# Keys projected first: a new hand-written order of the operations, and smaller tiles for the first transposes

## The chip, the core and the metric

The kernel runs on one core of a Trainium2 chip. TensorE (PE in the profile) does matrix products and transposes, VectorE (DVE) and ScalarE (ACT) elementwise work, GpSimd (POOL) elementwise work from memory alone, and SyncE (SP) issues most DMAs; ACT issues a few. Each engine runs its own instructions in order and waits on semaphores for the others. The metric is device microseconds of one execution; lower is better.

## The reference

A transformer block over `x` of 2048 tokens by 512 features, in bfloat16, with a conditioning vector `c`:

```python
mod = (_silu(c) @ w_mod).reshape(c.shape[0], 6, 1, -1)      # sa, ca, ga, sb, cb, gb
h = _layernorm(x) * (1 + ca) + sa
x = x + ga * _A_ref(h, A_wqkv, A_wo)
h = _layernorm(x) * (1 + cb) + sb
x = x + gb * _B_ref(h, B_w1, B_b1, B_w2, B_b2)
```

`_A_ref` is attention with 32 heads of 16: each token sees 8 positions, itself and every second token before it (window 8, dilation 2), with a softmax over the 8. `_B_ref` normalises once more and mixes tokens: `gelu(h^T w1 + b1) w2 + b2`, with `w1` 2048 by 1792 and `w2` 1792 by 2048.

## The kernel before

**Order.** The kernel first describes its work as a graph of named operations (`add`, `add_any`, lines 51 to 85), each with the engines that can do it. `schedule()` then emits them in the order of one long text, `ORDER` (line 180). A suffix picks the engine: `:a` ACT, `:d` DVE, `:p` POOL; without one the first alternative holds. `:q` splits a matmul into four of 32 output columns, `:s` skips. So the text fixes the order on every engine and on SP's queue. An operation that waits holds up whatever stands behind it on its engine, and a DMA waiting on SP holds up all later DMAs of SP. The text also hands out buffers: six PSUM tiles (`ps=6`, line 271), four large product buffers (`big`) and five `vD` buffers.

**Tiling.** The 16 token tiles of 128 are worked in five chunks of 2, 4, 4, 4 and 2 tiles (`SIZES`): chunk 0 is tiles 0 and 1, chunk 1 tiles 2 to 5, chunk 2 tiles 6 to 9.

**Loads and modulation.** `ld_x0`, `ld_x1` load one tile (128 KB), `ld_x_1_2` and its like two (256 KB). `ld_wmod1` and `ld_wmod0` (512 KB each) bring the columns for `ca` and `sa`; `modcols1` (PE) and `a1col` (DVE) make 1 + ca, `modcols0` (PE) and `sab` (DVE) make sa. `ld_wmod2` to `ld_wmod5` bring the other four parts, which `modrow`, `mrows` and `ld_row0` to `ld_row3` spread over the partitions. `ld_wqkv0`, `ld_wqkv1`, `ld_wqkv2` load the weights of queries, keys and values, 512 KB each.

**Layer norm.** `ln1s<tile>` takes a tile's statistics (DVE, one instruction of 0.6 us in a row of them; on ACT four instructions), `ln1v` aggregates them, `rstd1_<chunk>`, `rste1_` (ACT) and `nb1_` (DVE) give scale and shift, `n1_<tile>` normalises.

**Queries, keys, values.** For chunks 0 and 1 PE transposes the normalised tiles (`tr0_*`, `tr1_*`), and a copy `hT<chunk>_<k>` with the factor 1 + ca brings each block of 128 features into `hT`. These two chunks use the raw weights. Chunks 2 to 4 are transposed by DMA (`xt<tile>`) straight into `hT`, and use weights that were scaled by 1 + ca (`wsc<t>_<k>`, on DVE, ACT or POOL). There are two `hT` buffers: chunk 2 overwrites chunk 0's. The projections are `qkv<chunk>_<t><j>` with t = 0 for queries, 1 for keys, 2 for values; chunks 0 and 4 do two j in one group, so they have six groups and the others twelve. `ev<chunk>_<t><j>` copies a group out of PSUM; queries and values get a bias made from `sab` and the raw weights by `qvb0` and `qvb1` (PE) and `qvb_cp0`, `qvb_cp1` (DVE). Keys have no bias.

**Attention.** `qk<chunk>_<dlo>` (DVE) multiplies queries with eight shifted keys, 4096 products per partition (2048 for chunks 0 and 4); `red` (PE) sums them; `max`, `sub`, `exp`, `esum`, `rcp`, `rcq`, `smB` are the softmax. `a2_<chunk>_<jj>` and `vd<chunk>_<dhi>` are DMAs that rearrange the softmax and the values. `pv<chunk>_<dq>` (DVE) multiplies them, `pvacc` (PE) sums, `oev` copies. `halo_v` carries 16 values over to the next chunk.

**Second half.** `wo<tile>` (PE) and `x1_<tile>` apply `wo` and the residual; `n2`, `aff`, `afb` are the second norm with its scale and shift (DVE), `ln3s`, `ln3v`, `nb3`, `h3` the third. `mlp1_<part>_<f>_<s>` multiplies w1 with h3, which is possible as soon as the first `h3` tiles are there; `padd`, `park`, `gelu` close it, and `mlp2_<tile>`, `fin<tile>`, `st_out<tile>` finish the output.

**At the start.** PE runs matmuls on `ident` or on loaded tiles whose results nobody reads (`warm0` to `warm7`, lines 526 to 535); `WARM` gives their number, `GATE` the tile for which each waits.

The lines that make the transposes and the copies behind them:

```python
            KG = min(KT, 1024 // C)
            for k0 in range(0, KT, KG):
                s_ = _Slot("ps")
...
                        for sl in range(nt):
                            nc.tensor.transpose(trp[:, k2 * C + sl * P: k2 * C + (sl + 1) * P],
                                                h3[:, t0 + sl, (k0 + k2) * P:(k0 + k2 + 1) * P], ident[:])
```

C is the chunk's number of tokens, 256 or 512, so a PSUM tile holds four feature blocks of chunk 0 or two of chunk 1.

Of the kernel before, what the change touches and what calls it, by code (L numbers as in the profile page):

```python
# [190 lines left out]
qkv1_02 rste1_3 qkv1_21 smB0 ev1_02 ln1s14:a qkv2_00 a2_0_3 qkv2_10 red1_0 ev2_00 red1_1 a2_0_1 qk1_2 ln1v14 red1_2
ev2_10 modrow nb1_3 rstd1_4 wsc2_2:a red1_3 qkv1_22 qk2_0 vd0_0 qkv2_11 n1_11 n1_10:p max1 wsc2_1:a ev1_23 mrows
qkv1_20 a2_0_2 a2_0_0 rste1_4 ld_wo2 vd0_2 halo_v1:a ev1_22 vd0_3 biascols sub1 vd0_1 ev1_21 qkv2_03 pv0_0 pvacc0_0
ev1_20 exp1 ev2_11 ld_row2 pv0_2 nb1_4 esum1:q rcp1 rcq1 qkv2_01:q pv0_3 pvacc0_2 red2_0 n1_12 pvacc0_3 ev2_03
qkv2_13:q ld_row0 pv0_1 pvacc0_1 ev2_01 smB1 wsc2_3:a ev2_13 woq_s qkv2_12 qkv2_02 oev0_0 qkv2_22 oev0_2 ld_row1 wo0
qk2_1 wo1 ev2_12 red2_1 n1_13 vd1_3 ev2_02 x1_0 qkv2_20:q x1_1 biascols_cp qk2_3 qk2_2 ln2q0 qkv2_23:q red2_2 ln2q1
xt10 vd1_2 a2_1_0 red2_3 a2_1_3 n1_14 qkv2_21:q a2_1_1 a2_1_2 ev2_20 ln2m0 pv1_2 ev2_23 xt11 xt12 xt13 qkv3_02:q vd1_0
qkv3_11:q ln2w0 pvacc1_2 ev2_21 pv1_3 qkv3_10 rstd2_0 n1_15 rste2_0 nb2_0 qkv3_01 n2_0 max2 vd1_1 oev1_2 ev2_22 ev3_10
qkv3_13 ev3_02 n2_1:p aff0 xt14 pv1_0 ev3_11 qkv3_00 halo_v2 afb0 ev3_01 pv1_1 sub2 exp2 pvacc1_0 ev3_00 oev1_0
qkv3_20:q ev3_20 esum2:q pvacc1_3 rcp2 oev1_3 pvacc1_1 oev1_1 qk3_1 qkv3_12 rcq2 ev3_13 vd2_0 qkv3_03 ln3s1:a ev3_03  # L200
ev3_12 smB2 xt15 qkv4_10 ev4_10 ln3s0:a wo3 wo5 ld_w1_0_0 wo4 qk3_0 halo_v3:a x1_5 qk3_3 x1_4 red3_0 wo2:q x1_3
qkv4_20:q ln2q3 ln3v0 vd2_2 a2_2_0 vd2_3 qk3_2 ln3v1 x1_2 ln2q4 ln2m2 rstd3_0 ln2q5 a2_2_3 a2_2_2 a2_2_1 ln2q2
qkv4_00:q pv2_3 red3_1 qkv3_23:q vd2_1 ln2w2 red3_2 ev4_20 rstd2_2 rste3_0 qkv4_12:q ev4_12 rste2_2 qkv3_22:q pvacc2_3
red3_3 pv2_0 nb2_2 qkv4_02:q ev3_23 ev3_22 pv2_1 n2_2 ld_w1_0_512 qkv4_22:q ev4_00 pvacc2_1 pvacc2_0 n2_4 max3 sub3:q
# [6 lines left out]
mlp1_0_6_0:q oev3_0 mlp1_0_7_2:q mlp1_0_6_2:q pvacc3_2 n2_8:p mlp1_0_5_0:q mlp1_0_5_2:q oev3_2 pvacc3_1 max4 pv3_3
n2_7 vd4_1 vd4_2 ld_row3 park0_5 n2_6 aff6 mlp1_0_10_0:q oev3_1 mlp1_0_8_2:q sub4:q pvacc3_3 exp4 oev3_3 mlp1_0_10_2
esum4:d rcp4 ld_w1_0_1408 wo13 park0_6 wo12 afb6 rcq4 x1_13:d smB4 wo11 a2_4_2 wo10 x1_12:d x1_11:d ln3s7:a ln3s9:a
ln3s6 ln3s8 mlp1_0_11_0 ln3v7 mlp1_0_9_0 ln3v6 ln2q11 ln3v8 mlp1_0_9_2 ln3v9 vd4_3 mlp1_0_11_2 x1_10:d rstd3_6 rste3_6
nb3_6 h3_9:d a2_4_0 ln2q12 h3_7 a2_4_1 ln2m10 h3_8:d ln2q10 h3_6:d a2_4_3 mlp1_0_12_0 mlp1_0_12_2 mlp1_0_7_6 pv4_1
mlp1_0_8_6 park0_7 ln2w10 mlp1_0_9_6 ld_w2_4 mlp1_0_10_6 ln2m12 ln2q13 rstd2_10 pv4_0 pv4_2 park0_8 ld_w2_1 rste2_10
nb2_10 ld_w1_0_1664 ln2w12 pv4_3 pvacc4_0 n2_11 n2_10:d aff10 afb10 pvacc4_2 ln3s11 rstd2_12 pvacc4_1 oev4_0
mlp1_0_11_6:q pvacc4_3 park0_9 oev4_2 mlp1_0_12_6 rste2_12 nb2_12 wo14 park0_10 ln3s10:a n2_13:p wo15 mlp1_0_13_0
x1_14:d ln2q14 mlp1_0_13_2 big_done n2_12:d ln2m14 ld_w1_1_0 mlp1_0_13_6 ld_w1_1_640 park0_11 x1_15:d ln2w14 aff12
ln2q15 ln2m15 ln2w15 rstd2_15 rstd2_14 afb12 rste2_14 ln3v10 ln3v11 rstd3_10 rste3_10 ln3s13 nb2_14 mlp1_1_1_6 nb3_10  # L220
# [824 lines left out]
```

## Time and profile before

| | |
|---|---|
| median of 3 runs | 196.76 us (196.35 to 197.0) |
| the profiled execution | 196.38 us, of which the span 194.7 us |
| busy share of the span: PE, DVE, ACT, POOL | 96%, 83%, 63%, 13% |
| instructions | 4386 |
| HBM read, written | 22.03 MB, 2.10 MB |
| granted TensorE clock | 1.00 throughout |

All operations go through one helper, so nearly every row of the profile names line 131; tiles tell them apart. `big<-q_sb,k_f` is a product `qk`, `big<-a2sb,vD` a product `pv`, `psS<-hT,wst` or `psS<-hT,h` a projection with raw weights, `psS<-hT,w_qkv` one with scaled weights, `psS<-ident,h` a transpose, `psS<-sc,big` the modulation columns, `psS<-sab,wst` the query bias, `st<-xx` a statistic, `psS<-h,wst` the first MLP product. A row of the timeline has its start, its length, engine, operation, output and inputs, shapes, and the number of instructions merged; in brackets is how long the engine was idle before it, and what released it. PEld is the loading of weights into PE, which overlaps PE.

### The profile page before, as it was taken

Reading aid. Unit: us, or ns where it says so; the run is one execution under the profiler, and the core shown is the slowest. Engines: PE = TensorE matmul, PEld = TensorE weight load, DVE = VectorE, ACT = ScalarE, POOL = GpSimd, SP = SyncE. Lnnn points to the kernel's source line nnn. Section 1 sums busy time; section 2 is a strip of 40 time slices with the busy share of each in tenths; the row PEclk is TensorE's granted clock in tenths of the full one; section 3 lists DMA queues with packets and bytes.
Section 4 is the critical chain, followed back from the end, with each engine's and each line's share of the span. In section 5 each row is a group of like instructions: output and inputs, shape, how many; then the busy total and the mean of one; then the engine's idle time right before and its main releaser. Section 6 shows DMA issues by size and latency. Waiting matters only on the chain.

```text
span 194.7 us, 4386 instructions
## 1 busy us (share of the span) xinstructions
...
## 2 busy tenths in 40 slices
...
GB/s 169 320 364 254 231 183 164 268 219 178 226 152 262 187 236 209 29 107 388 200 271 71 146 231 258 329 340 236 319 22 30 148 27 0 210 90 56 92 83 81
DMA packets 55369, 35.94 MB, mean 185 GB/s; under 512 B 24628, under 2 KB 52788, under 8 KB 55348
## 3 DMA queue, kind: packets, MB, share of 16 engines
...
HBM read 22.03 MB, written 2.10 MB: 124 GB/s over the span
## 4 chain that ended last, share of the span: by engine, by line
PE 83%; DMA 6%; DVE 6%; SPq 2%; ACT 1%; issue 1%; POOL 0%; ACTq 0%
PE psS L131 79%; PE psL L131 3%; DVE big L131 2%; DMA vD<-v_sb 2%; DMA w_qkv<-in_B_w_dram 2%; DMA xx<-in_A_x_dram 2%; SPq L131 2%; DVE st L131 2%; DVE h L131 1%; DVE m L131 0%; DVE mv L131 0%; ACT xx L131 0%; ACT v_sb L131 0%; ACT o_sb L131 0%; POOL v_sb L131 0%
## 5 line engine op out<-in xcount | busy, mean ns | idle before, releaser
L131 PEld LDWEIGHTS <-wst 128*128 128x128 bf16 (+1 forms) x536 | 35.7, 100 | 32.1 <-issue 1.5
L131 PE MATMUL psS<-h,wst 128*32 128x512 bf16 (+1 forms) x374 | 51.0, 379 | 0.0
L131 DVE TENSOR_TENSOR big<-a2sb,vD 128x4096 bf16<-128x4096 bf16 (+1 forms) x20 | 36.9, 1857 | 0.6 <-DMA vD<-v_sb 0.3
L131 DVE TENSOR_TENSOR big<-q_sb,k_f 128x4096 bf16<-128x4096 bf16 (+1 forms) x20 | 36.5, 1855 | 0.0
L131 PE MATMUL psS<-hT,w_qkv 128*32 128x512 bf16 (+3 forms) x396 | 29.0, 334 | 0.1
L131 PEld LDWEIGHTS <-w_qkv 128*32 128x32 bf16 (+1 forms) x438 | 20.4, 107 | 15.4 <-issue 1.6
L131 DVE SCALAR_TENSOR_TENSOR h<-psS,bcol,rows_bc 128x512 f32<-128x512 f32 x15 | 11.3, 750 | 19.0 <-PE psS L131 18.9
L131 POOL TENSOR_SCALAR h<-xx,rs,nb 128x512 bf16<-128x512 bf16 x12 | 15.2, 1273 | 90.0 <-DVE nb L131 84.1
L131 PE MATMUL psS<-gT,big 128*128 128x512 bf16 x112 | 25.0, 379 | 0.0
L131 PEld LDWEIGHTS <-big 128*128 128x128 bf16 x144 | 12.0, 97 | 13.8 <-DMA big<-in_w_mod_dram 0.6
L131 ACT ACTIVATE junk<-xx 128x512 bf16<-128x512 bf16 x26 | 16.3, 627 | 0.4
L131 PE MATMUL psS<-woq,o_sb 128*128 128x512 bf16 (+1 forms) x76 | 15.8, 379 | 0.0
L131 ACT ACTIVATE gT<-psS,bcol 128x512 bf16<-128x512 f32 x14 | 8.9, 685 | 8.1 <-DVE psS L131 7.9
L131 DVE TENSOR_TENSOR psS<-psS,gT 128x512 f32<-128x512 f32 x14 | 9.4, 695 | 5.2 <-PE psS L131 5.1
L131 ACT ACTIVATE h<-xx,nb,rs 128x512 bf16<-128x512 bf16 x15 | 12.0, 809 | 2.2 <-DVE nb L131 2.2
L131 PEld LDWEIGHTS <-group 128*32 128x32 bf16 x288 | 6.9, 96 | 11.0 <-DVE big L131 4.3
L131 PE MATMUL psS<-big,group 128*32 128x512 bf16 (+1 forms) x160 | 10.1, 338 | 2.0 <-DVE big L131 1.4
L131 PE MATMUL psS<-hT,wst 128*128 128x256 bf16 (+2 forms) x76 | 11.7, 335 | 0.0
L131 ACT ACTIVATE v_sb<-psS,qvb 128x512 bf16<-128x512 f32 (+1 forms) x20 | 11.1, 599 | 0.1
L131 DVE TENSOR_TENSOR h<-h,xx 128x512 bf16<-128x512 f32 x15 | 10.4, 692 | 0.7
L131 DVE TENSOR_TENSOR h<-h,rows_bc 128x1024 bf16<-128x1024 bf16 (+2 forms) x14 | 10.7, 761 | 0.2
L131 ACT ACTIVATE q_sb<-psS,qvb 128x512 bf16<-128x512 f32 (+1 forms) x18 | 10.7, 619 | 0.0
...
## 6 DMA issues: line engine op xcount, KB each, us to landing
...
```

The lines of the kernel that those rows point to most:

```text
L131: r = fn(*a, **k)
```

## The change

The order is written anew, three constants change with it, and nothing is added to or left out of what is computed. The two lists hold the same operations, but for three more transposing tiles. The core of the diff, cut to the start and to the stretch around the end of chunk 2's attention:

```diff
@@ -178,60 +178,61 @@
 ORDER = """
-ident halo0 ld_c cps act_table silu_exp silu_dve ld_x1 ln1s1 warm0 ld_x0 ln1s0 ln1v0 ln1v1 rstd1_0 ld_x_2_8 ld_x_1_2
-ld_x_1_4 ld_x_2_6 ld_wmod1 ln1s2 ln1s3 warm1 rste1_0 consts nb1_0 ln1v2 warm7 ln1s8:a ln1s5 ln1v8 ln1v3 ld_wmod0 warm3
-ln1v5 ln1s4 warm4 warm2 ln1s9:a ln1v9 warm6 ln1s7 ln1v4 ld_wqkv0 rstd1_1 modcols1 ln1s6 ld_wqkv1 n1_1:p rste1_1 nb1_1
-n1_0:p n1_4 ln1v7 tr0_0 ln1v6 n1_3:d a1col warm5 modcols0 rstd1_2 n1_2:d n1_5:p tr1_0 rste1_2 nb1_2 ld_x_3_12 ld_wqkv2
-tr1_2 n1_7:p sab qvb0 ld_b2 hT0_3 ld_x_4_14 hT0_1 n1_6:p hT0_0:d ld_x_3_10 hT0_2 ld_wmod2 hT1_2 hT1_1 qkv0_00 wsc1_1:a
-wsc0_2 hT1_0 qkv0_10 qkv0_02 qkv0_12 wsc0_0 ev0_10 hT1_3:d qvb_cp0 ev0_00:d qkv0_20 qkv0_22 ln1s13 ld_wo3 n1_9:p
-wsc0_1:a xt6 ev0_02 ld_wmod5 ln1s12 qkv1_03 qk0_0 qvb1 ev0_12 wsc1_0:a wsc1_3:p qkv1_13 qk0_1 red0_0 qk0_3 red0_1
...
+ident warm1 ld_c cps ld_x_1_2 warm0 ld_x_1_4 warm5 ld_x0 act_table consts warm7 silu_exp ln1s2:a silu_dve ln1s5 ln1s4
+ln1v5 ln1v2 ln1s3 ln1v4 ld_x1 ln1v3 ln1s1 ln1s0:a ln1v0 warm4 rstd1_1 rste1_1 nb1_1 n1_3:p ln1v1 ld_x_2_6 rstd1_0
+ld_x_2_8 ln1s8 rste1_0 nb1_0 ld_wmod1 n1_1:p n1_5 warm2 ld_wqkv1 ld_x_3_12 n1_0 modcols1 ld_wmod0 ld_wqkv0 n1_2:p
+tr0_0 ln1s6 ln1s9 ln1s7 ld_x_3_10 tr0_2 ld_wqkv2 a1col wsc1_0:p wsc1_3:p n1_4:d hT0_0 warm6 ld_x_4_14 tr1_3 hT0_3:d
+tr1_1 ld_wo0 wsc1_2:p hT0_1 hT0_2:d hT1_1 wsc1_1:p ln1v6 tr1_0 ln1v9 ln1v8 ln1v7 hT1_3:d ln1s12 tr1_2 hT1_0 rstd1_2
+qkv0_10 rste1_2 qkv0_12 nb1_2 modcols0 hT1_2 n1_8:d sab qkv1_10 n1_7:p ld_wo2 qvb0 halo0 ev0_10 ev0_12 qkv0_00 n1_6:d
+ln1s11 ln1s13:a qkv0_02 n1_9:p wsc0_1:a qkv0_20 ld_wmod3 qvb_cp0 ln1s10:a ln1v12 ev0_02 ev0_00:d ev1_10 wsc0_3:a
+qkv0_22 xt6 ln1v11 qkv1_00 qk0_0 qkv1_02 qk0_1 qk0_3 ld_wmod4 ev1_00 wsc0_2:p ln1v10 red0_0 qk0_2 qk1_0 ln1s15:a
+ev1_02 ln1s14:a ln1v13 ld_b1 qkv1_03:q ld_wmod5 red0_1 ln1v15 red0_2 red0_3 mask qkv1_12 max0 ev1_12 qvb1 qvb_cp1
+qkv1_13 qkv1_01 ev1_03 xt9 qk1_2 ev1_13 sub0 ev0_20 exp0 ev0_22 xt8 xt7 rstd1_3 qkv1_23 ev1_01 qkv1_21 esum0 qkv1_11
+ld_wmod2 ln1v14 rcp0 qk1_3 rste1_3 qkv1_22 wsc0_0:p rcq0 ev1_11 smB0 ev1_21 ld_wo3 qk1_1 halo_v1:d rstd1_4 ld_wo1
+rste1_4 ld_b2 qkv2_00 ev2_00 qkv2_10 red1_0 modrow a2_0_1 nb1_4 nb1_3 n1_10:p vd0_3 a2_0_0 a2_0_3 ev2_10 a2_0_2 red1_1
...
-n2_3 pv2_2 n2_5:p aff2 nb3_0 qkv3_21:q oev2_1 pvacc2_2 oev2_3 h3_1:p afb2 ev4_22 exp3 oev2_0 h3_0:p oev2_2 esum3
-ld_w2_0 wo7 rcp3 ld_w1_0_896 rcq3 smB3 ev3_21 a2_3_1 wo9 ln3s4 ln3s5 a2_3_2 wo6 ln3s3 ev4_02 ln3v4 ln3s2:a ln3v2 x1_7
-ln3v3 ln3v5 a2_3_3 mlp1_0_2_0 x1_6 a2_3_0 wo8 vd3_0 rstd3_2 rste3_2 vd3_2 qk4_0 mlp1_0_8_0 mlp1_0_4_0 x1_9 mlp1_0_1_0
...
+vd3_3 max3 pvacc2_0 pv2_3 qkv4_12:q ev4_12 aff2 ln3v1 ln3v0 sub3:q qkv4_00:q afb2 exp3 pvacc2_3 oev2_1 oev2_0 esum3
+oev2_3 rstd3_0 rcp3 rste3_0 rcq3 nb3_0 ev4_00 smB3 ld_w1_0_896 wo8 h3_0:p a2_3_2 ln3s5 ln3s3:a wo7 ln3s2 ln3s4 a2_3_1
+h3_1:p ln3v3 x1_8 x1_7 ln3v5 wo6 ln3v4 ln3v2 rstd3_2 rste3_2 a2_3_0 mlp1_0_1_0 x1_6 qk4_2 wo9 x1_9 nb3_2 qk4_0
...
-    WARM=(1, 3, 8, 1, 1, 3, 2, 1),
+    WARM=(2, 2, 1, 1, 8, 2, 1, 1),
     GATE=(None, None, 1, 8, 2, 4, 6, None),
...
-            KG = min(KT, 1024 // C)
+            KG = min(KT, 512 // C)
```

What it does, engine by engine:

- SP: the first loads are tiles 2 to 5, then 0 and 1, 6 to 9, `ld_wmod1`, `ld_wqkv1`, tiles 12 and 13, `ld_wmod0`, `ld_wqkv0`, tiles 10 and 11, `ld_wqkv2`. Behind `xt6` come `ld_wmod4`, `ld_b1`, `ld_wmod5`, `xt9`, `xt8`, `xt7`; before, these were `ld_wmod5`, `ld_wmod3`, `xt8`, `xt7`, `xt9`. Among the `a2_0` and `vd0` transfers `ld_wo2` no longer stands.
- PE: a transposing tile holds two feature blocks of chunk 0 or one of chunk 1. Then come `qkv0_10`, `qkv0_12`, `modcols0`, `qkv1_10`, `qvb0`, `qkv0_00`; before, `modcols0` ran ahead of `tr1_0`, and `qvb0`, `qkv0_00`, `qkv0_10` followed the transposes.
- DVE: statistics of tiles 5, 4, 3, 1, 8, 6, 9, 7 (before 1, 0, 2, 3, 5, 4, 7, 6), then `a1col` and `n1_4`. `ln1s11` and `ln1s12` stand ahead of `qk0_0`.
- Moved between engines near the start: to POOL `n1_3`, `n1_2` and `wsc0_2`, `wsc0_0` (from DVE), `wsc1_0`, `wsc1_1` (from ACT); to DVE `n1_4`, `ln1s8`, `ln1s9`, `hT0_3`, `hT0_2`, `halo_v1` (from ACT), `n1_8`, `n1_6` (from POOL); to ACT `ln1s2`, `ln1s0`, `ln1s13`, `hT0_0` (from DVE), `n1_5`, `n1_0` (from POOL).
- Later, chunk 2's value products run in the order `pv2_2`, `pv2_1`, `pv2_0`, `pv2_3` instead of `pv2_3`, `pv2_0`, `pv2_1`, `pv2_2`; `pv2_2` stands behind three products `qk3` after `smB2`, as `pv2_3` did before. `nb3_0` stands behind `afb2` instead of ahead of it. Some statistics and normalisations of the second half change engine, `n2_12` and `n2_15` go to POOL, and the order of the MLP products, the output tiles and the store queues is another.
- The number of warm-up matmuls goes from 20 to 18.

More of the change, by code (lines that the diff above doesn't have):

```diff
@@ L191 @@
[L191 to L204, printed above, removed]
-n2_3 pv2_2 n2_5:p aff2 nb3_0 qkv3_21:q oev2_1 pvacc2_2 oev2_3 h3_1:p afb2 ev4_22 exp3 oev2_0 h3_0:p oev2_2 esum3
@@ L211 @@
[L211 to L220, printed above, removed]
@@ new lines @@
+xt12 wo0 wo1 ld_row2 ev2_22 qkv2_21 x1_0 x1_1 qkv2_20 ln2m0 red2_1 ln2q1 ln2q0 pv1_2 red2_2 ev2_20 red2_3 ln2w0
+rstd2_0 rste2_0 ev2_23 qkv3_10:q qkv3_02:q pv1_3 nb2_0 max2 n1_15 ev2_21 n2_1 pvacc1_2 qkv3_00 qkv3_01 oev1_2 ld_row1
+vd1_0 ev3_10 pv1_0 biascols_cp n2_0:p aff0 ev3_01 vd1_1 sub2 qkv3_12 ev3_00 exp2 xt14 ev3_12 qkv3_11 pvacc1_3 ev3_02
+esum2:q ev3_11 oev1_3 rcp2 pvacc1_0 rcq2 pv1_1 afb0 qkv3_03:q ev3_03 qkv3_21:q smB2 halo_v2 vd2_3 pvacc1_1 oev1_0
+qkv3_13 vd2_1 vd2_0 oev1_1 wo5 ln3s1:a wo2 qkv3_22 wo3 halo_v3:a ln3s0:a x1_2 x1_5 ev3_22 qk3_0 qk3_1 x1_3 wo4 qk3_2
```

55 lines of the change are left out of this document (35 added, 20 removed).

## The prediction

> **What bounds the kernel now.** First the page, then the stretches, then the chain of waits. The columns of the stretches are start:end, length, then busy time (instructions) of PE, PEld, DVE, ACT and POOL, the granted clock and the DMA share.
>
> ```profile
> span 194.7 us, 4386 instructions
> ```
>
> ```profile
> 16.30:80.00 63.70, 61.55 (x841) 34.22 (x839) 63.33 (x58) 60.97 (x143) 6.36 (x5) 1.00 0.80 204
> 80.00:126.90 46.90, 46.84 (x442) 22.00 (x443) 46.24 (x97) 41.22 (x111) 8.90 (x8) 1.00 0.76 210
> 126.90:192.10 65.20, 65.11 (x330) 30.92 (x328) 39.43 (x60) 10.09 (x15) 0.00 (x0) 1.00 0.44 127
> ```
>
> ```profile
> 2.20 3.50 DMA xx<-in_A_x_dram
> ...
> 7.75 0.37 DVE mv L131 x3
> ...
> 8.84 0.60 DVE st L131
> ...
> 80.02 7.70 PE psS L131 x46
> ...
> 192.04 0.29 DVE h L131
> ```
>
> The chain (start, length, what) ends in PE and one last add. The stretches say why. From 16.3 to 80 DVE is idle for 0.37 of 63.7 us while PE is idle for 2.15: DVE's queue of products sets the pace there, and PE has no other work, since the first MLP matmuls need h3. From 80 on PE never stops. So there are two clocks: DVE from its first product (qk0_0) to the last value product of chunk 2, then PE to the end.
>
> ```profile
> 10.37 0.38 DVE L131 TENSOR_SCALAR h<-xx,mv,rs 128x512 bf16<-128x512 bf16 x1
> ...
> 14.46 0.69 DVE L131 TENSOR_TENSOR q_sb<-psS,qvb 128x512 bf16<-128x512 f32 x1
> ...
> 16.26 4.62 DVE L131 TENSOR_TENSOR big<-q_sb,k_f 128x2048 bf16<-128x2048 bf16 x4
> ...
> 31.85 2.29 DVE L131 TENSOR_TENSOR big<-q_sb,k_f 128x4096 bf16<-128x4096 bf16 x1
> ...
> 36.71 1.23 DVE L131 TENSOR_TENSOR big<-a2sb,vD 128x2048 bf16<-128x2048 bf16 x1 [0.30 <-DMA vD<-v_sb]
> ...
> 77.69 2.28 DVE L131 TENSOR_TENSOR big<-a2sb,vD 128x4096 bf16<-128x4096 bf16 x1
> ...
> 81.14 1.23 DVE L131 TENSOR_TENSOR h<-h,rows_bc 128x2048 bf16<-128x2048 bf16 x1
> 82.28 0.68 DVE L131 TENSOR_TENSOR lsb<-lsb,rb 128x1024 bf16<-128x1024 bf16 x1
> ```
>
> The last value product (pv2_2) ends at 79.97 and PE's pvacc2_2 starts at 80.02. By the two lists PE has the same matmuls left behind that point in both kernels, so the end moves by as much as that point moves, plus what PE waits later.
>
> **The change, part by part.** *Loads.* Sizes in order, in KB, before: 768 up to tiles 2/3, 1792 up to the first modulation weights, 2304 the second, 2816 the query weights, 3328 the key weights. After: 512 up to tiles 4/5, 1792 the first modulation weights, 2304 the key weights, 3072 the second modulation weights, 3584 the query weights.
>
> ```profile
> L131 SPq DMA_DIRECT2D wst<-in_A_wqkv_dram x2: 508/678/847, 4.8 to 5.4; - x2
> ...
> DMA to landing us min/median/max: 8.1/8.1/8.1
> ```
>
> ```profile
> 9.10 0.47 PEld L131 LDWEIGHTS <-big 128*128 128x128 bf16 x16 [0.32 <-DMA big<-in_w_mod_dram]
> ...
> 10.52 0.53 PEld L131 LDWEIGHTS <-big 128*128 128x128 bf16 x16 [0.25 <-DMA big<-in_w_mod_dram]
> ```
>
> 768 KB were there at 5.70 (the chain's DMA row), 1792 at 9.10, 2304 at 10.52 and 3328 at 5.4 + 8.1 = 13.5: about 0.73 us per 256 KB at the end of that. So the key weights come at 10.5 (3.0 earlier), the second modulation weights at 12.7, the query weights at 14.2. A product needs key and query. Both are there at 13.5 before and at 14.2 after, so the reordering by itself makes no product possible sooner; it only gives PE key work first.
>
> *Up to the first matmuls.* Tiles 4/5, statistics first after, land near 4.7 (5.70 less 256 KB at 0.85 us, the rate from 5.70 to 9.10, gives 4.85; loads go out at the same pace). DVE then runs eight statistics at 0.60, nine small ones at about 0.12 (the chain's three in 0.37), and n1_4, which the change moves onto DVE, at 0.38: 6.3 us, so n1_4 ends at 11.0 and chunk 1's transposes start there. Before, they started at 11.51. In tiles of half the size they are as many instructions; the first copies can start earlier, and six tiles fill the six PSUM buffers, of which the oldest are read by 11.5. Worth 0 to -0.3; taken at 0, as the transposes wait for n1_4.
>
> ```profile
> 10.61 0.54 PE L131 MATMUL psS<-sc,big 128*128 128x1 bf16 x16
> 11.51 1.07 PE L131 MATMUL psS<-ident,h 128*128 128x128 bf16 x16 [0.36 <-DVE h L131]
> 12.42 0.67 PE L131 MATMUL psS<-sab,wst 128*128 128x1 bf16 x16
> 12.95 3.73 PE L131 MATMUL psS<-hT,wst 128*128 128x256 bf16 x32
> 16.52 1.91 PE L131 MATMUL psS<-hT,h 128*128 128x256 bf16 x16
> ```
>
> *PE's order.* From these starts: 16 transposes 0.91, the query bias qvb0 0.53, one projection group 0.89 (four from 12.95 to 16.52), modcols0 0.45 (0.54 less the overlap with what follows). Before: qvb0 at 12.42, then the first query group. After: transposes to 11.9, two key groups to 13.7, modcols0 to 14.1 (its weights at 12.7), a key group of chunk 1 to 15.0, qvb0 to 15.5 (query weights at 14.2: 0.8 of cover), the query group to 16.4. Its copy on DVE (0.69) ends at 17.1. **qk0_0 starts at 17.1, against 16.26: +0.85.** Bounds: 16.6 if tiles 4/5 land 0.5 sooner, 17.9 if n1_4 and the copy meet POOL.
>
> *DVE's stream from qk0_0 to the end of chunk 2's last value product.* After it lacks ln1s11 (0.60) and two aggregates (0.2), done ahead of qk0_0, and the aggregates ln3v0 and ln3v1 (0.2), put behind; it gains halo_v1 (a small one, 0.12). Sum -0.9. That would cancel the late start, but for one gate on the way, qk2_0.
>
> ```profile
> 18.48 1.31 SPq L131 DMA_TRANSPOSE hT<-h  x1
> 19.83 1.12 SPq L131 DMA_DIRECT2D gT<-in_w_mod_dram  x2
> 21.07 3.85 SPq L131 DMA_TRANSPOSE hT<-h  x3
> ...
> 25.59 0.54 SPq L131 DMA_DIRECT2D b_t<-in_B_b_dram  x1
> ```
>
> ```profile
> 29.13 1.89 PE L131 MATMUL psS<-hT,w_qkv 128*128 128x512 bf16 x8
> ...
> 31.06 0.60 ACT L131 ACTIVATE k_f<-psS 128x512 bf16<-128x512 f32 x1
> ```
>
> *The gate at qk2_0.* Chunk 2's transposing DMAs overwrite chunk 0's hT, so SP's queue stands at xt6 until the last chunk 0 group, which ends at 18.4 before (16.52 + 1.91) and at 16.4 + 3 x 0.89 = 19.1 after. Everything behind xt6 on SP, loads included, waits with it. Then two modulation loads come in both kernels, and the change puts ld_b1 (0.54) in between: the last transpose is 0.7 + 0.6 = 1.3 later. PE's side: ahead of qkv2_00 it has one group (0.89) and modcols0 (0.45) more, and started 0.5 earlier: 29.13 + 0.8 = 29.9. By the transposes it is 30.4 at most; I take 30.1, +1.0. Key evacuation ended 0.19 ahead of qk2_0, so qk2_0 moves by 0.8, to 32.65; DVE itself would be there at 32.2. From there the stream is 0.3 shorter, and the wait of 0.30 at 36.71 should go, as ld_wo2 no longer stands ahead of the vD copies on SP. **The last value product of chunk 2: +0.8 - 0.3 - 0.3 = +0.2** (+0.5 if that wait stays).
>
> *Into the MLP.* nb3_0 moves behind afb2, 1.2 us later.
>
> ```profile
> 7.18 1.51 POOL L131 TENSOR_SCALAR h<-xx,rs,nb 128x512 bf16<-128x512 bf16 x2 [3.65 <-DVE mv L131]
> ...
> 32.11 2.67 POOL L131 TENSOR_SCALAR h<-xx,rs,nb 128x512 bf16<-128x512 bf16 x1 [15.74 <-DVE nb L131]
> ...
> 81.35 2.92 POOL L131 TENSOR_SCALAR h<-h,rs,nb 128x512 bf16<-128x512 bf16 x2 [4.07 <-DVE nb L131]
> ```
>
> ```profile
> 84.32 0.59 PE L131 MATMUL psS<-h,wst 128*128 128x512 bf16 x2
> ```
>
> POOL's pair ended at 84.27 and PE used it at 84.32. After, it starts near 82.4 on the old time axis and takes 1.5 to 2.2 (smB3 alone beside it): 83.9 to 84.6. PE waits 0 to 0.3; taken 0.1.
>
> The Trainium skill ("SBUF — State Buffer", Who interferes with whom) calls the port that DVE and GpSimd share an exclusive lock, taken by a DVE instruction with two SBUF inputs. The rows agree: one POOL operation took 2.67 us beside a product, two took 1.51 beside statistics. By that rule the change, which gives POOL four more weight scalings (two of key, two of query weights), would pay 0.7 us wherever one slips past qk0_0; my count puts them all before 17.
>
> *Free edits.* Warm-ups (18 for 20) run before 9.5, except one of 0.2 us placed mid-stream. Stores change queues (ACT, SP), but the last piece still has 128 columns and its add (0.29), store after it. Engine swaps of LN work behind 80 lie beside PE's 46.84 of 46.90; without that cover they cost what they are, 0.3 to 0.7 each.
>
> **Sum**: +0.2 +0.1, and 0.1 for half the doubt on the 0.30: +0.4 on the profiled execution's 196.38 (span 194.7, 1.7 around it) is 196.8. The median shown, 196.76, is 0.38 above that execution, so 196.8 to 197.2: I say 197.0. Own range 196.2 to 197.8.
>
> **Rivals.** *Slower: DVE comes too early to the softmax copies of chunk 2.*
>
> ```profile
> 62.10 0.68 DVE L131 TENSOR_TENSOR lsb<-lsb,rb 128x1024 bf16<-128x1024 bf16 x1
> ...
> 69.79 2.29 DVE L131 TENSOR_TENSOR big<-a2sb,vD 128x4096 bf16<-128x4096 bf16 x1
> ```
>
> Before, pv2_3 came 7.0 us after smB2; after, pv2_2 comes 6.6 after it, behind the same four copies and one vD transfer. Past 6.6 us each microsecond goes to DVE and then to PE, which has no filler yet. With 1 to 2 us late copies: 198.0 to 198.9, say 198.4. For: the 0.30 wait at 36.71 shows that such transfers do run late. Against: no wait at 69.79. Chance 0.26.
>
> *Faster: the start costs nothing.* With tiles 4/5 at 4.2 and qk0_0 at 16.6, chunk 0's hT is free near 18.6; if ld_b1 slips in beside it, qk2_0 is on time (31.9), the stream's -0.3 and -0.3 stay: 196.76 - 0.7, near 196.0. For: ACT is lighter there, two weight scalings fewer. Against: five PE slots ahead of the query group. Chance 0.23.
>
> *PE at half rate.*
>
> ```profile
> 2.56 2.31 PE L131 MATMUL psS<-ident 128*128 128x512 bf16 x5
> ...
> 9.96 0.81 PE L131 MATMUL psS<-xx,ident 128*128 128x512 bf16 x3
> ```
>
> Matmuls stand 0.43 apart at 2.56 and 0.22 apart at 9.96, at a granted clock of 1.00 throughout. After, PE pauses between 3.4 and 4.7, as its third warm-up waits for tile 4. If the slow rate lasts to 14, transposes and two groups (2.7 us) take twice as long: +2 on the gate, 199. The Trainium skill ("TensorE: Matmul & The Clock Gate", What's actually happening) has half rate until one busy window of some 3.4 us; the rows before agree, with one pause inside. After is busy from 4.7 to 9.6, so I give it 0.06.
>
> **How the numbers follow.** 0.3% (0.6 us) is about what a measurement can tell here. Forecast 0.45: same 0.31, slower 0.12, faster 0.02. The slower rival 0.26 and the half rate 0.06: slower. The faster one 0.23: faster. So faster 0.25, same 0.31, slower 0.44. The range from 195.6 to 198.8 leaves out the half rate and the ends of both rivals.
>
> **What would show it.** qk0_0 at 16.6 to 17.9; key projections ahead of the second modulation columns; xt6 issued near 19; qk2_0 near 32.6 with a DVE wait for ACT's k_f; no vD wait near 37; chunk 2's last value product ending 0 to 0.5 later; PE without a pause from there. Wrong if DVE waits for a2sb near 67, if POOL's operations of 2.7 us stand beside the first products, or if PE waits behind 84.

## The result, and the profile after

Before ran in 196.82 us (median of 4 runs on the same chip, 196.35 to 197.0), after in 199.51 us (198.75 to 200.78): a ratio of 1.0142, 95% interval 1.0111 to 1.0174. The change makes the kernel 2.7 us slower, and the prediction (197.0, range 195.6 to 198.8) was wrong. The profiled execution took 199.3 us with a span of 197.6, against 196.38 and 194.7. In u1_query, l1_no_a2, l2_no_b1 and l3_no_vd4 below one run each was in a slower state, over 1.5% above the kernel's fastest, and is left out of the times.

The two clocks of the prediction can be laid over both profiles. These are the stretches of each kernel between the same four events: the first product qk0_0, qk2_0, the end of chunk 2's last value product, and PE's end. First before, then after; the columns are start:end, length, busy time (instructions) of PE, PEld, DVE, ACT and POOL, granted clock, DMA share and GB/s.

```profile
16.26:31.85 15.59, 15.59 (x142) 9.10 (x144) 15.59 (x20) 15.30 (x38) 0.11 (x1) 1.00 0.87 199
31.85:79.97 48.12, 46.00 (x707) 25.16 (x702) 47.75 (x40) 45.68 (x105) 6.29 (x4) 1.00 0.78 206
79.97:192.04 112.07, 111.94 (x770) 52.92 (x770) 85.64 (x155) 51.34 (x125) 8.90 (x8) 1.00 0.57 162
```

```profile
17.22:33.01 15.79, 15.31 (x134) 8.60 (x138) 15.19 (x19) 14.20 (x37) 0.43 (x1) 1.00 1.00 200
33.01:81.69 48.68, 45.60 (x633) 24.10 (x625) 47.59 (x35) 45.41 (x100) 3.94 (x4) 1.00 0.71 206
81.69:194.95 113.26, 112.45 (x776) 53.03 (x776) 84.78 (x157) 51.47 (x127) 10.30 (x9) 1.00 0.58 156
```

The 2.91 us are three pieces: 1.16 up to qk2_0, 0.56 from there to the last value product (48.68 - 48.12), 1.19 behind it (113.26 - 112.07). DVE has less work up to the last value product than before (15.19 + 47.59 = 62.78, against 63.34), but stands idle 1.69 us of it, against 0.37. These rows of DVE's timeline in after are its waits there, and one wait behind them:

```profile
33.01 2.47 DVE L131 TENSOR_TENSOR big<-q_sb,k_f 128x4096 bf16<-128x4096 bf16 x1 [0.60 <-ACT k_f L131]
...
55.89 2.29 DVE L131 TENSOR_TENSOR big<-a2sb,vD 128x4096 bf16<-128x4096 bf16 x1 [0.64 <-DMA vD<-v_sb]
...
69.25 2.29 DVE L131 TENSOR_TENSOR big<-a2sb,vD 128x4096 bf16<-128x4096 bf16 x1 [0.46 <-DMA a2sb<-lsb]
...
113.81 1.22 DVE L131 TENSOR_TENSOR big<-a2sb,vD 128x2048 bf16<-128x2048 bf16 x1 [0.60 <-DMA vD<-v_sb]
```

These are qk2_0, the third value product of chunk 1 (pv1_0), pv2_2 and pv4_2. The chain of waits of after (start, length, what) names the transfers behind them, and one more for PE:

```profile
22.98 1.20 SPq L131
24.23 1.27 SPq L131
25.55 4.81 DMA hT<-h
30.36 0.09 issue
30.45 1.91 PE psS L131 x8
32.38 0.60 ACT k_f L131
...
65.99 3.14 DMA a2sb<-lsb
...
108.81 4.98 DMA vD<-v_sb
...
129.23 6.90 DMA wst<-in_B_w_dram
136.18 58.75 PE psS L131 x299
194.95 0.29 DVE h L131
```

PE's own row behind that w1 load, in its timeline:

```profile
136.18 6.00 PE L131 MATMUL psS<-h,wst 128*128 128x512 bf16 x27 [0.40 <-DMA wst<-in_B_w_dram]
```

Before, 79% of the chain was PE on its PSUM tiles and 6% DMA; now it is 47% and 12%. SP's queue shows why the pv1_0 copy is late. Before, vd1_0 and vd1_1 went out right behind the three transposes:

```profile
43.94 3.91 SPq L131 DMA_TRANSPOSE hT<-h  x3
47.91 2.35 SPq L131 DMA_DIRECT2D vD<-v_sb  x2
```

After, ld_row2 and ld_row1 stand in between, and the pair goes out 2.6 later, 1.35 of it because the transposes ahead are later themselves, 1.28 for the two loads:

```profile
45.29 3.91 SPq L131 DMA_TRANSPOSE hT<-h  x3
49.25 1.24 SPq L131 DMA_DIRECT2D rows_bc<-mrows  x2
50.53 1.26 SPq L131 DMA_DIRECT2D vD<-v_sb  x2
...
108.16 0.61 SPq L131 DMA_DIRECT2D w_qkv<-in_B_w_dram  x1
108.81 0.78 SPq L131 DMA_DIRECT2D vD<-v_sb  x1
```

The last two rows are the same at pv4_2: its copy vd4_2 goes out right behind ld_w2_1, a load of 448 KB, and takes 4.98 to land.

The start itself came as forecast. The first product's rows in after:

```profile
16.40 0.69 DVE L131 TENSOR_TENSOR q_sb<-psS,qvb 128x512 bf16<-128x512 f32 x1 [0.30 <-PE psS L131]
...
17.22 3.50 DVE L131 TENSOR_TENSOR big<-q_sb,k_f 128x2048 bf16<-128x2048 bf16 x3
```

### The profile page after: what moved, and what is told of

It is laid out like the page before. It is cut to its first block, busy times and chain, and to the rows that moved or that the text cites. A ratio compares the mean times of both kernels' runs of the same rounds, so it can differ in the third digit from the quotient of the medians.

```text
span 197.6 us, 4250 instructions
## 1 busy us (share of the span) xinstructions
PE 188.3 (95%) x1661; PEld 94.9 (48%) x1661; DVE 160.0 (81%) x246; ACT 124.3 (63%) x293; POOL 25.1 (13%) x48
## 4 chain that ended last, share of the span: by engine, by line
PE 47%; DVE 21%; DMA 12%; issue 11%; SPq 4%; ACT 3%; DVEq 0%; ACTq 0%
PE psS L131 47%; DVE big L131 12%; SPq L131 4%; DMA wst<-in_B_w_dram 3%; DVE h L131 3%; DMA vD<-v_sb 3%; DMA hT<-h 2%; DMA a2sb<-lsb 2%; DVE m L131 2%; DMA xx<-in_A_x_dram 2%; DVE lsb L131 1%; DVE st L131 1%; ACT h L131 1%; DVE mv L131 1%; ACT v_sb L131 1%
## 5 line engine op out<-in xcount | busy, mean ns | idle before, releaser
L131 PE MATMUL psS<-hT,w_qkv 128*32 128x256 bf16 (+2 forms) x360 | 29.3, 323 | 0.5 <-DMA hT<-h 0.5
L131 POOL TENSOR_SCALAR h<-xx,rs,nb 128x512 bf16<-128x512 bf16 x12 | 14.2, 1188 | 90.5 <-DVE nb L131 70.2
L131 DVE SCALAR_TENSOR_TENSOR h<-psS,bcol,rows_bc 128x512 f32<-128x512 f32 x15 | 11.2, 748 | 17.6 <-PE psS L131 17.6
L131 ACT ACTIVATE junk<-xx 128x512 bf16<-128x512 bf16 x28 | 17.6, 630 | 1.8 <-DMA xx<-in_A_x_dram 1.4
L131 PE MATMUL psS<-woq,o_sb 128*128 128x512 bf16 x64 | 15.9, 379 | 0.0
L131 ACT ACTIVATE h<-xx,nb,rs 128x512 bf16<-128x512 bf16 x16 | 12.6, 811 | 1.3 <-DVE nb L131 1.3
```

The source lines that it names most:

```text
L131: r = fn(*a, **k)
```

## The experiments

The theory after this reading: the loss is a sum of transfers that SP issues too late for the engine that now wants them. Two rivals: the gates hand a delay on, so that mending one gains nothing; or keys first, with its later first product, costs the 2.7 us by itself. A kernel is named by its label; its ratio is to runs of before on the same chip. The last three columns, in us, are from its own profile: start of the first product, start of qk2_0 (DVE's idle time ahead of it), end of the last value product of chunk 2.

| label | made from | median us | ratio (95%) | first | qk2_0 | last pv2 ends |
|---|---|---|---|---|---|---|
| before | | 196.82 | | 16.26 | 31.85 (0) | 79.97 |
| after | | 199.51 | 1.0142 (1.0111 to 1.0174) | 17.22 | 33.01 (0.60) | 81.69 |
| e1_vd1 | after | 199.13 | 1.0126 (1.0099 to 1.0154) | 17.61 | 33.75 (0.89) | 82.11 |
| e2_xt | after | 200.30 | 1.0199 (1.0135 to 1.0262) | 18.08 | 33.29 (0) | 83.67 |
| e3_late | after | 198.89 | 1.0120 (1.0062 to 1.0179) | 17.69 | 33.89 (1.01) | 82.16 |
| e4_all | after | 199.48 | 1.0138 (1.0106 to 1.0170) | 18.28 | 33.55 (0.07) | 82.70 |
| e5_fit | after | 199.50 | 1.0152 (1.0111 to 1.0194) | 17.47 | 32.83 (0.07) | 83.11 |
| p1_keys | before | 198.36 | 1.0077 (1.0057 to 1.0098) | 18.15 | 33.74 (0) | 81.85 |
| t1_tiles | before | 196.76 | 1.0003 (0.9981 to 1.0024) | 16.78 | 32.52 (0) | 80.73 |
| x1_start | before | 199.04 | 1.0108 (1.0078 to 1.0139) | 17.16 | 33.09 (0) | 81.59 |
| x2_rest | both | 199.69 | 1.0153 (1.0103 to 1.0204) | 16.44 | 34.46 (0) | 82.63 |
| e6_mend | after | 197.21 | 1.0029 (1.0004 to 1.0053) | 17.91 | 33.06 (0) | 80.39 |
| l2_no_b1 | e6 | 197.71 | 1.0032 (1.0009 to 1.0056) | 17.53 | 34.25 (1.25) | 81.59 |
| l3_no_vd4 | e6 | 197.56 | 1.0039 (1.0021 to 1.0057) | 17.63 | 33.09 (0.26) | 80.42 |
| l4_no_vd1 | e6 | 197.81 | 1.0051 (1.0026 to 1.0075) | 17.56 | 33.39 (0.61) | 81.55 |
| e7_query_up | e6 | 197.53 | 1.0027 (1.0004 to 1.0050) | 16.89 | 33.20 (0.49) | 80.72 |
| e8_loads_up | e7 | 197.19 | 1.0019 (0.9997 to 1.0040) | 16.91 | 32.80 (0.07) | 80.13 |
| b1_order | before | 196.31 | 0.9972 (0.9953 to 0.9991) | 16.77 | 32.37 (0) | 80.37 |

**One place at a time.** The first edit of the order text (a token is a line here):

```diff
+vd1_0 vd1_1
 ld_row2
...
 ld_row1
-vd1_0
...
-vd1_1
```

> The kernel after, with the two value copies vd1_0 and vd1_1 ahead of ld_row2 and ld_row1 on SP. Late-transfer theory (the 2.7 us are a sum of transfers that SP issues too late): DVE's wait of 0.64 for vD at 55.89 goes, all behind it comes 0.6 sooner, 198.9 against 199.5. Rival (the waits hand the delay on: what one gate gives back, the next one takes): the wait goes, a wait of about the same size grows at pv2_2 or behind it, 199.5. Rival (keys first itself costs it): 199.5.

The wait at pv1_0 is gone. But qk2_0 and pv2_2 waited longer, 0.89 and 0.94, and the median fell by 0.4, inside the intervals. Nor need the edit be what removed the wait: in e3_late below, which leaves these copies where they were, it is gone too, because DVE comes to pv1_0 later there as well (55.97; in after it was free at 55.25). DVE in e1_vd1 at pv2_2, and in e3_late at pv1_0:

```profile
69.67 2.29 DVE L131 TENSOR_TENSOR big<-a2sb,vD 128x4096 bf16<-128x4096 bf16 x1 [0.94 <-DMA a2sb<-lsb]
```

```profile
55.97 2.28 DVE L131 TENSOR_TENSOR big<-a2sb,vD 128x4096 bf16<-128x4096 bf16 x1
```

So this run shows no gain, as the first rival has it, and leaves the price of the vd1 pair open until l4_no_vd1.

```diff
 xt6
+xt9 xt8 xt7
...
 ld_wmod4
...
 ld_b1
...
 ld_wmod5
...
-xt9
...
-xt8 xt7
...
 ld_wmod2
```

> The kernel after, with xt9, xt8 and xt7 right behind xt6 on SP, so ahead of the modulation loads 4 and 5 and of ld_b1. Late-transfer theory: the transposes land by 27, qkv2_00 on PE no longer waits for hT (0.64 lost at 30.45 in after), qk2_0 moves from 33.01 to about 32.4, 198.9. Rival (PE's own late start sets the gate): the wait for hT goes, qk2_0 stays within 0.15 of 33.0, 199.4.

DVE's wait at qk2_0 went, 15.2 us behind the first product instead of 15.8, and the kernel still became slower. The modulation loads were now late, and PE stood at modrow, with the reductions of chunk 1's products queued behind it. PE and then DVE in e2_xt:

```profile
35.07 0.39 PE L131 MATMUL psS<-wst,sc 128*32 128x512 bf16 x1 [1.90 <-DMA wst<-in_w_mod_dram]
```

```profile
37.46 1.22 DVE L131 TENSOR_REDUCE m<-psL 128x128 bf16<-128x1024 f32 x1 [1.88 <-PE psL L131]
```

The third edit concerns the stretch behind chunk 2:

```diff
+vd4_2
 ld_w2_1
...
-vd4_2
...
+ld_w1_2_0
 ld_w1_1_1408
...
-ld_w1_2_0
```

with mlp1_1_5_6, 5_10 and 6_10 ahead of 3_6 and 3_10 on PE.

> The kernel after, with vd4_2 ahead of ld_w2_1, and the second MLP sweep ordered so that ld_w1_2_0's buffer comes free sooner and it is issued ahead of ld_w1_1_1408. Late-transfer theory: DVE's wait of 0.60 at 113.81 and PE's of 0.57 at 136.18 go, together -1.0, 198.5. If only one of the two was on the path: -0.5, 199.0. Rival (PE behind 80 was not the place): no change, 199.5.

The wait at pv4_2 went, PE's wait for w1 only became smaller (0.31 at 134.88, against 0.40 at 136.18). From the last value product to the end it took 0.5 less than after, and the start was 0.5 later: 198.89, unclear by itself.

> All three edits together, and pv2_3 ahead of pv2_2 with vd2_2 behind the last a2 copy of chunk 2 (DVE's wait of 0.45 at 69.25). Late-transfer theory: -0.6 -0.6 -0.45 -1.0 = 196.8, level with before (196.8), the last value product of chunk 2 ending near 80.1. Rival (waits hand the delay on): no more than -1.2, 198.3 or above. Rival (keys first itself costs the 2.7): 198.5 or above.

All three edits, and the order pv2_3 ... pv2_2 with vd2_2 behind the last a2_2 copy: no gain. pv2_2's wait was gone, but the PE stall at modrow from the moved transposes was still there, DVE's wait for it being 1.63. Next came e5_fit, which also put modrow, mrows and ld_row0 behind the last vd0 copy, and left out the w1 edit:

```diff
 red1_0
-modrow
...
-mrows
...
-ld_row0
...
 vd0_1 pv0_2
+modrow mrows ld_row0
 qkv2_01
```

> After with the transposes and the vd1 copies moved as in the first two edits, vd4_2 ahead of ld_w2_1, pv2_3 ahead of pv2_2, and modrow, mrows and ld_row0 behind the last vd0 copy, so that PE doesn't stand at modrow for the modulation weights. Late-transfer theory in its new form (DVE's stretch is 62.7 us of work, and 1.7 of waits fill up whatever single edit is made): stretch 62.7 to 63.0, last value product near 80.3, PE 112.6 behind it: 197.2 to 197.6. Rival (another wait takes the room again): stretch 64.4, 199.2.

The stall at modrow went, and the row it makes was late for woq_s. DVE in e5_fit:

```profile
41.48 1.23 DVE L131 TENSOR_TENSOR woq<-woq,rows_bc 128x2048 bf16<-128x2048 bf16 x1 [2.70 <-DMA rows_bc<-mrows]
```

Without these 2.70 the stretch from qk2_0 on would have been 47.6, below before's 48.1, which showed where to go next.

**Four places together.** e6_mend touches neither transposes nor modrow:

```diff
-ld_b1
...
 xt7
+ld_b1
...
+vd1_0 vd1_1
 ld_row2
...
-vd1_0
...
-vd1_1
...
-vd2_2
 a2_2_0
-pv2_2 pvacc2_2 oev2_2
+vd2_2 pv2_3 pvacc2_3 oev2_3
...
-pv2_3
+pv2_2
...
-pvacc2_3
+pvacc2_2
...
-oev2_3
+oev2_2
...
+vd4_2
 ld_w2_1
...
-vd4_2
```

> After with four moves, none of them at the start or at modrow: ld_b1 behind xt7, vd1_0 and vd1_1 ahead of ld_row2, pv2_3 ahead of pv2_2 with vd2_2 behind the last a2 copy, vd4_2 ahead of ld_w2_1. Late-transfer theory: from qk2_0 to the last value product of chunk 2 47.5 us as in the run that moved modrow, less its wait at woq (after 48.7, before 48.1); behind it 112.2 (after 113.2); with the first product at 17.2 to 17.7: 196.7 to 197.3. Rival (each gate takes what another gives): 198.8 or above.

197.21, inside the expectation: by the ratios (1.0142 and 1.0029), each to before on its own chip, some 2.2 us of the loss are back. Its stretches, then DVE's rows in order of time: qk2_0, then pv1_0, the first value product of chunk 2, and pv4_2, none with a wait.

```profile
17.91:33.06 15.15, 15.04 (x132) 8.41 (x136) 15.15 (x19) 14.26 (x37) 0.00 (x0) 1.00 0.77 188
33.06:80.39 47.33, 45.08 (x628) 24.24 (x625) 47.31 (x36) 45.30 (x100) 6.35 (x4) 1.00 0.73 215
80.39:192.62 112.23, 111.45 (x767) 53.07 (x776) 84.83 (x156) 51.53 (x127) 10.40 (x9) 1.00 0.58 158
```

```profile
33.06 2.29 DVE L131 TENSOR_TENSOR big<-q_sb,k_f 128x4096 bf16<-128x4096 bf16 x1
...
55.14 2.28 DVE L131 TENSOR_TENSOR big<-a2sb,vD 128x4096 bf16<-128x4096 bf16 x1
...
67.95 2.28 DVE L131 TENSOR_TENSOR big<-a2sb,vD 128x4096 bf16<-128x4096 bf16 x1
...
111.83 1.22 DVE L131 TENSOR_TENSOR big<-a2sb,vD 128x2048 bf16<-128x2048 bf16 x1
```

DVE's idle time up to the last value product is 0.02 us (after 1.69), and the stretch behind it is within 0.2 of before's. Then each place was put back alone.

> The mended kernel (e6) with the order of pv2_2, pv2_3 and vd2_2 as in after. If pv2_2 comes too early to its a2 and vD copies: DVE waits 0.45 to 0.95 at pv2_2 (the four copies take 7.1 to 7.6 us from smB2, DVE's work before pv2_2 6.6), 0.5 to 0.9 above e6: 197.7 to 198.1. If not: 197.2.

197.41 (ratio 1.0034, 1.0007 to 1.0061).

> The mended kernel with ld_b1 between the modulation loads 4 and 5 again. If its 0.6 of SP's time sets qk2_0: DVE waits 0.6 to 0.9 for k_f there, 197.8 to 198.1. If PE's own start sets it: 197.2.

> The mended kernel with vd4_2 behind ld_w2_1 again. If a copy that queues behind a 460 KB load lands too late: DVE waits 0.5 to 0.6 at pv4_2 near 112, PE 0.5 behind it, 197.7. If not: 197.2.

> The mended kernel with vd1_0 and vd1_1 behind ld_row2 and ld_row1 again. If they are late for DVE now that it is on time: a wait of about 0.6 at the third value product of chunk 1, 197.8. If not: 197.2.

In the last three profiles the wait came back, at qk2_0, pv4_2 and pv1_0. One DVE row of l2_no_b1, l3_no_vd4 and l4_no_vd1 each:

```profile
34.25 2.29 DVE L131 TENSOR_TENSOR big<-q_sb,k_f 128x4096 bf16<-128x4096 bf16 x1 [1.25 <-ACT k_f L131]
```

```profile
112.50 1.23 DVE L131 TENSOR_TENSOR big<-a2sb,vD 128x2048 bf16<-128x2048 bf16 x1 [0.56 <-DMA vD<-v_sb]
```

```profile
56.28 2.29 DVE L131 TENSOR_TENSOR big<-a2sb,vD 128x4096 bf16<-128x4096 bf16 x1 [0.66 <-DMA vD<-v_sb]
```

The medians lie 0.2 to 0.6 above e6_mend's, but on another chip. By the ratios, each to before on its own chip, the four lie 0.1, 0.1, 0.2 and 0.4 us above it (l1, l2, l3, l4), and every interval overlaps with e6_mend's. So the four moves together are shown by times, and no single share is; those rest on the waits in the profiles.

- *pv2_2.* The wait stands in the five profiles of the table with after's order there (after, e1_vd1, e2_xt, e3_late, x2_rest: 0.46 to 0.94) and in none of the eight made from after with pv2_3 first.
- *pv4_2.* It stands in the five with the copy behind ld_w2_1 (after, e1_vd1, e2_xt, x2_rest, l3_no_vd4: 0.52 to 0.67) and in none of the eight with the copy ahead.
- *pv1_0.* It stands in after (0.64) and l4_no_vd1 (0.66). In e2_xt, e3_late and x2_rest the copies are as late, but DVE comes later too and doesn't wait.
- *qk2_0.* DVE waited 0.60 to 1.25 with ld_b1 as in after (after, e1_vd1, e3_late, l2_no_b1), and 0, 0.26 and 0.61 without (e6_mend, l3_no_vd4, l4_no_vd1). In l2_no_b1 the three transposes went out 1.7 later than in e6_mend (23.89 for 22.22). ld_b1 itself is some 0.6 of that, and the load behind it took SP 1.43. That run, 198.58, is the slowest of the nine. In l4_no_vd1 the profile names ACT's copy of a value group, and no transpose, as what released PE's group ahead of qk2_0. So this gate has more than one cause.

**The parts of the change alone.** Keys first, in before's order:

```diff
-ld_wmod0
+ld_wqkv1
...
-ld_wqkv0
+ld_wmod0
...
-ld_wqkv1
+ld_wqkv0
...
-modcols0
...
-sab qvb0
...
+qkv0_10 modcols0 sab qvb0
 qkv0_00
...
-qkv0_10
```

> Before with keys first alone: key weights behind the first modulation weights, query weights last, one key projection of chunk 0 ahead of modcols0 and qvb0. Tiles, x loads and all behind as in before. If keys first costs what the first product waits for the query weights: qk0_0 0.3 to 0.8 later than 16.26, 197.0 to 197.5. If it is free: 196.6. If it is the main cause of after: 198 or more.

198.36, the time that the expectation had set for keys first as the main cause. DVE reaches sab early and stands there until PE has made the second modulation columns (modcols0), which now come behind the key group on PE; the profile shows no wait for their weights. The scaling of query weights and the last copy into hT stand behind sab on DVE. DVE and PE in p1_keys, then its stretches:

```profile
14.52 0.16 DVE L131 CAST sab<-psS 128x4 bf16<-128x4 f32 x1 [1.79 <-PE psS L131]
```

```profile
13.94 0.54 PE L131 MATMUL psS<-sc,big 128*128 128x1 bf16 x16
```

```profile
18.15:33.74 15.59, 15.38 (x138) 8.57 (x139) 15.59 (x21) 14.60 (x35) 0.00 (x0) 1.00 0.64 165
33.74:81.85 48.11, 45.99 (x707) 25.20 (x702) 47.74 (x40) 45.70 (x105) 6.29 (x4) 1.00 0.79 206
81.85:193.95 112.10, 111.98 (x770) 52.91 (x770) 85.74 (x156) 51.34 (x125) 8.90 (x8) 1.00 0.57 162
```

All three lengths are before's to 0.03: where the order behind the first product stays, its delay of 1.89 goes through to PE's end one for one (1.9 later in the profile; 1.5 by the medians).

Undoing keys first in after:

```diff
-ld_wqkv1
+ld_wmod0
...
-ld_wmod0 ld_wqkv0
+ld_wqkv0 ld_wqkv1
...
+modcols0 sab qvb0 qkv0_00
 qkv0_10
```

> After with keys first alone undone: loads in before's order (second modulation weights, query, key weights), modcols0, qvb0 and the query group ahead of the key group on PE. Theory: DVE has its own work up to 16.4, so the first product comes at most 0.3 sooner and may come later where it now waits for the key weights: 199.0 to 199.8. Rival (keys first costs in after what it costs in before, 1.5): 198.0.

Slower still: 200.72 in three runs, ratio 1.0185 (1.0142 to 1.0229). So undoing keys first alone gains nothing inside after. That the order around it was laid out for keys first is the likely reason, and not shown. The half tiles alone, in before (`KG = min(KT, 512 // C)` and the tokens tr0_2, tr1_1, tr1_3):

> Before with the half transposing tiles alone. As forecast, worth 0 to -0.3: the copies start earlier, the transposes stay behind n1_4: 196.5 to 196.8. Rival (a sixth tile waits for a buffer, two more PSUM tiles cost the projections time): 197.1 or more.

No change, as forecast. Two mixed kernels joined the orders at qk0_0.

> The start of after (everything up to the first product qk0_0: loads of tiles 4/5 first, key weights ahead, half transposing tiles), then before's order unchanged; of the other loads ahead of xt6 those of before. Theory A (the new start itself delays the clock, and before's order behind it has no slack): first product at 17.2 to 17.7, last value product of chunk 2 about 1.0 later than in before, 197.6 to 198.0. Theory B (the start is caught up, the loss lies in the new order behind it): 196.6 to 196.9. Theory C (the start carries all of it): 199.0 or more.

Theory C by the time. The first product was 0.90 late, and the delay grew behind it: 1.24 at qk2_0, 1.62 at the end of chunk 2, and the wait for the a2 copies of chunk 4 grew from 0.26 to 0.97. DVE in x1_start:

```profile
111.81 1.23 DVE L131 TENSOR_TENSOR big<-a2sb,vD 128x2048 bf16<-128x2048 bf16 x1 [0.97 <-DMA a2sb<-lsb]
```

> The start of before up to qk0_0 (first product near 16.3), then after's order. Theory A: DVE's stretch from the first product to the last value product of chunk 2 is 64.4 as in after, so that point comes near 80.7, and PE's waits behind it stay: 198.3 to 198.8. Theory B: no better than after, 199.3 or more. Theory C: 196.8.

This one doesn't answer its question: at the seam DVE waited 2.02 us for a tile of x that before's loads bring later. Neither order fits the other's start. By x1_start alone the start would carry most of the loss. But e6_mend keeps that start, has its first product at 17.91, and is 2.2 us faster than after: a late start costs what the order behind it can't hide.

**The start in the mended kernel.**

```diff
-qkv1_10
...
 qkv0_00
+qkv1_10
```

> The mended kernel (e6) with chunk 1's key projection qkv1_10 behind the query projection qkv0_00 on PE, so that qvb0 and the query group come up to 0.87 sooner, if the query weights (landing 14.5 to 14.8) are there. If the late first product passes on to the end one for one, as before's order passed it on: DVE's wait of 0.30 to 0.70 for the query group goes, the first product comes 0.3 to 0.65 sooner, 196.6 to 196.9. Rival (the gate at qk2_0, set by SP's transposes, takes it): 197.2.

```diff
 ld_wmod3
+ld_wmod4 ld_wmod5
...
 xt6
...
-ld_wmod4
...
-ld_wmod5
```

> The kernel before this one (e7: e6 with qkv1_10 behind the query group) with ld_wmod4 and ld_wmod5 ahead of xt6, in the 5.9 us in which SP's queue stands there, so that the four transposes follow one another. If the transposes set qk2_0 (33.20 in e7, with 0.26 of PE's wait for hT and 0.49 of DVE's for k_f): PE has no wait for hT, DVE's wait goes to 0 to 0.2, qk2_0 at 32.7 to 32.9, 197.0 to 197.2 against 197.5. Rival (PE and ACT set it with their own work): qk2_0 stays at 33.2, 197.5.

In e7_query_up the first product came 1.0 sooner than in e6_mend and qk2_0 not at all: its expectation missed, the gate took everything. In e8_loads_up the four transposes follow one another, and qk2_0 comes 0.4 sooner, as expected. DVE in e7_query_up, and in e8_loads_up SP and DVE:

```profile
33.20 2.58 DVE L131 TENSOR_TENSOR big<-q_sb,k_f 128x4096 bf16<-128x4096 bf16 x1 [0.49 <-ACT k_f L131]
```

```profile
19.50 5.30 SPq L131 DMA_TRANSPOSE hT<-h  x4
```

```profile
32.80 2.29 DVE L131 TENSOR_TENSOR big<-q_sb,k_f 128x4096 bf16<-128x4096 bf16 x1
```

By time the three kernels can't be told apart (1.0029, 1.0027, 1.0019). In this order qk2_0 is set by SP's transposes and PE's two groups behind them, and a first product up to about 1 us later is hidden ahead of it.

**A version ahead of both.** The same care, given to before:

```diff
-ld_wo2
...
 vd0_1
+ld_wo2
...
-vd4_3
...
 a2_4_3
+vd4_3
```

> Before with two moves on SP: ld_wo2 behind the four vd0 copies (after does that too), vd4_3 behind the four a2 copies of chunk 4. If the wait of 0.30 at 36.71 is on the path and nothing behind it takes the room, and PE's 0.3 near 112 goes: 196.3 to 196.5. Rival: no change, 196.8.

196.31, a ratio of 0.9972 (0.9953 to 0.9991): 0.3% ahead of before, and the fastest kernel here. Which of the two moves does it is not shown. In its profile (197.03, the slowest of its ten runs) the wait of 0.30 at 36.71 is gone, but DVE stands 0.2 longer elsewhere, ahead of pv2_3, and the stretch from qk2_0 to the last value product is 48.00 us for 48.12. The wait of 0.26 for the a2 copies of chunk 4 is gone too.

## Why the prediction was wrong, by its own steps

- *PE's order.* First product forecast at 17.1, seen at 17.22. Key groups stood ahead of modcols0, xt6 went out at 19.06 as said. The steps are right; that the profile lies so close is in part luck, as ten other profiles with this start have it at 17.16 to 18.28, six of them behind 17.6.
- *The gate at qk2_0.* Right in kind, too small: 33.01 for 32.65. The prediction named 30.4 as the bound by the transposes and took 30.1, between that and PE's own count of 29.9. PE's group started at 30.45, released by the last transpose, which landed 4.8 after its issue. The three transposes went out 1.9 later than before (22.98 for 21.07), not 1.3, as ld_wmod5 alone took SP 1.21. The gate is 0.36 of the missing 2.5 us; ld_b1 is among its causes by the waits listed above.
- *DVE's stream.* Work forecast 0.9 shorter; 62.78 for 63.34 in after (0.56), where qk2_0 took 2.47 instead of 2.29; 62.46 in e6_mend (0.88), where no wait is left.
- *The wait of 0.30 at 36.71 goes.* Right in after. What it is worth is not shown: in b1_order most of it came back ahead of pv2_3.
- **The step that failed: "The last value product of chunk 2: +0.8 - 0.3 - 0.3 = +0.2."** It was +1.72. The sum let DVE run through from qk2_0 on, and followed only one transfer, the vD copies behind ld_wo2, past SP's queue. The change moves others too: the vd1 pair to behind two ld_row transfers (0.64), and pv2_2 to 6.6 us of work behind smB2 (0.46). From qk2_0 on the stream's work was 0.16 shorter (47.59 for 47.75), not 0.3, since qk2_0 itself ran 0.18 longer beside a POOL operation. So 0.64 + 0.46 + 0.14, and 0.36 at the gate, make the 1.5 that were missing, to within 0.1.
- *The slower rival.* "DVE comes too early to the softmax copies" was the right mechanism and too large: 0.46 us in after, and up to 0.94 in the four other profiles with that order, not 1 to 2. It stood beside the forecast as an alternative at 0.26, and belonged into the sum.
- *Into the MLP.* The 0.1 taken for nb3_0 did not come: PE's first MLP matmul is 4.25 behind its first sum of the last value product (81.75 to 86.00), against 4.30 before (80.02 to 84.32).
- *"PE without a pause from there."* Wrong by the same kind of step: vd4_2 behind a 448 KB load (DVE 0.60, absent wherever the copy went first) and a w1 load that PE waits for (0.40 at 136.18). The second is not settled: e1_vd1 and e6_mend have the same w1 loads without that wait. Of the 1.19 behind chunk 2 the remaining 0.2 stands in e6_mend too (112.23 for 112.07); its cause is open.
- *The faster rival* needed a first product at 16.6 and a free gate; neither came.
- *Half tiles, free edits.* Half tiles: right (t1_tiles). The edits called free were not run alone; the 0.2 just named is what may be theirs behind chunk 2.
- *POOL's scalings.* All were done ahead of the first product, the last at 17.12, in 0.67 us each, so none slipped beside a product. Two POOL rows of the same size show what the sentence on the shared port was about. The first, in after, began while DVE stood idle; the second, in e6_mend, began beside qk2_0:

```profile
32.58 0.76 POOL L131 TENSOR_SCALAR h<-xx,rs,nb 128x512 bf16<-128x512 bf16 x1 [15.46 <-ACT q_sb L131]
```

```profile
33.27 2.73 POOL L131 TENSOR_SCALAR h<-xx,rs,nb 128x512 bf16<-128x512 bf16 x1 [15.87 <-ACT k_f L131]
```

The product beside the second took its usual 2.29; the one that began 0.43 behind the first, qk2_0 in after, took 2.47. By the Trainium skill ("SBUF — State Buffer", Who interferes with whom) the later of the two waits for the whole of the other; the 2.73 agree with that, and the 2.47 go the same way.

- *PE at half rate* did not come where it was priced: the 16 matmuls of the two key groups took 1.91 from 11.71 on in after, the pace that before had. Ahead of that the slow pace lasts differently: the nine warm-ups on x took 4.04 from 5.58 on in after, and 2.52 from 5.62 on in e4_all.
- *The chances.* Slower had 0.44, more than the same (0.31) or faster (0.25); the number, 197.0, and the range gave that too little weight.
